# Softmax denominators transposed before the reciprocal, and one rounding of V moved to GpSimd

## The chip, the cores and the metric

The kernel runs on one core of a Trainium2 chip. The metric is the device time of one execution in microseconds (us); the number compared is the median of several executions. TensorE is called PE here, VectorE DVE, ScalarE ACT, GpSimd POOL, and SyncE, whose queue issues most DMAs, SP.

## What is computed

Rotary attention, then a gated feed-forward, then a second feed-forward with SoLU and layer norm. Only the attention is touched by the change:

```python
q_rot, k_rot = rotate(q), rotate(k)                      # batch 2, 8 heads, 576 rows, 64 columns
scores = q_rot @ k_rot.T / sqrt(64)
attn = exp(scores - max(scores))
attn = attn / (sum(attn) + 1e-09)
x = attn @ v                                             # then 1152 tokens x 512
x = (x @ w_a) * (x @ w_b) @ w_out
h = x @ moe2_w_in                                        # SoLU, layer norm, @ moe2_w_out
```

All of it is float32. Products run as float32r passes over a high part (the value rounded) and a low part (the rest) of each operand, so every operand is split by a copy ("high") and a subtraction ("low").

## The kernel before

**Tiling.** Two heads make a head pair; there are eight pairs, `u` = 0 to 7. A pair has nine blocks of 128 query rows: four of the first head, four of the second, and one (number 4) with the last 64 rows of both. For each block PE makes the scores `s` against all 576 keys (`qk`, L327), DVE takes the negated row maximum `nm` (L336), ACT takes the exponential `e` and adds up each row into one column of `sums[u]`, a tile of 128 partitions by 9 (L344), PE transposes `e` into `t` (L354), ACT copies it rounded into `pT` (L368) and DVE writes the low part (L372). The last 64 key rows are transposed apart (`t4A`, `t4R`, `t4B`, L378, evacuated at L386 and L390). Four products of `pT` with `V` (`pv`, L403), each evacuated by ACT (L410) and DVE (L417), give the pair's output `x0`, not yet divided.

**Division.** `rs_dve` (L422, L423) adds 1e-9 to the sums and takes their reciprocals on the 128 x 9 tile, in place. `rs_pe` (L427) transposes the result into PSUM, so that it has 9 partitions by 128. `rs_copy` (L430 to L446) copies it to SBUF on ACT as `rr`, and, for pairs 0 to 6, writes it to DRAM and reads it back three times, spread over the partitions, as `rb`; POOL then multiplies `x0` by `rb` (L468, L469) and takes the low part (L477). For the last pair `rb_pe` (L449) spreads `rr` with small products instead, and DVE multiplies (L483).

**V.** `v_hi` (L244) rounds the 128 x 640 tile `vraw` into the high half of `V` on DVE (L233); `v_lo` (L249) writes the low half on POOL (L251). POOL also does the rotation of keys and queries (L219 to L224), the low part of the keys (`k_lo`, L242), and the multiplications by `rb`.

**Order.** Nothing is scheduled by a tool: each part of a pair has a position in slots, nine slots a pair, in the tables `PLAN`, `FIRST`, `SECOND` and `THIRD`, where the last three override the first for pairs 0, 1 and 2. The parts are issued in the order of `9 * u + position`, and every engine works through its own instructions in that order. `rs` has three positions, for the sums' reciprocals, the transposition and the copy; `v_hi` and `v_lo` have one each. The last pair also has the first products of the feed-forward between its parts (`ab`, L579, at the positions in `AB`).

**Buffers.** The tiles with tag `o` in the pool `ps_o` share two PSUM buffers in rotation: the transpositions of queries and keys (`qtkA`, `qtqA`, `qtR`, `qtkB`, `qtqB`), `t4A`, `t4R`, `t4B`, `rs` and the four `pv`. Each of them waits until the one before the last has been evacuated. The scores `s` have two buffers, the transposed `t` two, and for the last pair the two tiles of `rb_pe` are taken from the buffers of `t`.

Of the kernel before, what the change touches and what calls it, by code (L numbers as in the profile page):

```python
# [15 lines left out]
ALU = mybir.AluOpType  # L16
# [4 lines left out]
B, H, S, D = 2, 8, 576, 64  # L21
NT, DM, DF1, DF2 = B * S, 512, 1536, 1024
P = 128
NP = H // 2
NU = B * NP
NB = 9
# [5 lines left out]
# When the parts of a head pair's work are issued, in slots from the pair's first one: each slot has  # L32
# the products of one block of queries, and the other parts are spread between them.
# [26 lines left out]
HI = {"k": "act", "v": "dve", "x": "pool", "l0": "pool", "l5": "dve", "q0": "dve", "q5": "dve", "r": "act"}  # L60
# [3 lines left out]
# A float64's high word is sign, 11 bits of exponent and 20 of mantissa. Read as a float32, the high  # L64
# words of the float32 range's ends are these two.
# [8 lines left out]
class Weights:  # L74
    """Float64 weights, as raw words in `raw` [P, n, 2], turned into float32 in `t` [P, n] and its
    float32r high and low parts in `w` [P, 2, n]; `scale` is a factor for each partition."""
# [4 lines left out]
    def pack(self, steps=range(5)):  # L81
        """The float32 value, cut to 24 bits; 0 below float32's range."""
        eng, t = self.nc.vector, self.t
        lo, hi = self.raw[:, :, 0], self.raw[:, :, 1]
        for step in steps:
            if step == 0:
                self.nc.scalar.activation(_raw(t), _raw(hi), AF.Abs)  # L87
            elif step == 1:
                eng.tensor_scalar(_raw(t), _raw(t), LOW_END, HIGH_END, op0=ALU.max, op1=ALU.min)  # L89
            elif step == 2:  # L90
                eng.tensor_scalar(t, t, 3, 0x3FFFFFFF, op0=ALU.logical_shift_left, op1=ALU.bitwise_and)  # L91
            elif step == 3:
                eng.scalar_tensor_tensor(t, hi, -(1 << 30), t, op0=ALU.bitwise_and, op1=ALU.bitwise_or)  # L93
            else:
                eng.scalar_tensor_tensor(t, lo, 29, t, op0=ALU.logical_shift_right, op1=ALU.bitwise_or)  # L95
# [12 lines left out]
def attention_gated_ffn_solu_ffn(ctx: ExitStack, tc, q, k, v, wa, wb, wo1, wi2, wo2, gln, rope_cs, out):  # L108
    """Products run as float32r passes over exact high and low halves of every float32 operand."""
    nc = tc.nc  # L110
# [12 lines left out]
    # ---- weights, in the order of their use: wa|wb by 128 columns, wo1 by 128 columns and half its  # L123
    # rows, wi2 by 128 rows and half its columns, wo2 (times the layer norm's factors) by 128 rows
# [39 lines left out]
    # ================= attention =================  # L164
# [14 lines left out]
    def load(u, nm_, parts="ABR", eng=nc.sync):  # L179
        """Queries or keys [P, 9, D]: 4 blocks of the first head's first 512 rows (row 4p + c is in  # L180
        block c), both heads' last 64 rows, 4 blocks of the second head's. Queries go into the second
        half of a tile [P, 9, 2, D], which will have them twice."""
        b, h0 = u // NP, 2 * (u % NP)
        if nm_ == "k":
# [3 lines left out]
            t = kraw[u]  # L188
# [55 lines left out]
    def v_hi(u):  # L244
        t = at.tile([P, 2, 5, 2, D], F32R, tag="V", name=f"V{u}")
        copy(HI["v"], t[:, :, :, 0, :].rearrange("p h c d -> p (h c) d"), vraw[u].rearrange("p h c d -> p (h c) d"))
        V[u] = t
# [173 lines left out]
    def rs_dve(u, key):  # L421
        nc.vector.tensor_scalar(sums[u], sums[u], 1e-9, None, op0=ALU.add)  # L422
        nc.vector.reciprocal(sums[u], sums[u])  # L423

# [5 lines left out]
    def rs_copy(u, key):  # L430
        rr = st.tile([NB, P], F32, tag="rr", name=f"rr{u}", bufs=2)
        copy(HI["r"], rr, po[u, key][0:NB, 0:P])
# [16 lines left out]
    def rb_pe(u):  # L449
        """1 / sum at every row of x0, by products with copies of the identity's columns."""  # L450
# [38 lines left out]
    # ---- what the start needs beside the plan  # L489
# [5 lines left out]
    def start():  # L495
# [19 lines left out]
        # the tensor engine's clock rises while it is busy: products of no use until the data is there  # L515
# [18 lines left out]
    for u in range(NU):  # L534
        plan = {key: tuple(9 * u + x for x in np.atleast_1d(pos)) for key, pos in PLAN.items()}
        for first, early in enumerate((FIRST, SECOND, THIRD)):
            if u == first:
                plan |= {key: tuple(9 * u + x for x in np.atleast_1d(pos)) for key, pos in early.items()}
# [22 lines left out]
        for keys, fns in (  # L561
            (("kA", "kB"), (qt_pe, qt_act)), (("qA", "R", "qB"), (qt_pe, qt_act, qt_dve)),
            (("t4A", "t4R", "t4B"), (t4_pe, t4_act, t4_dve)), (("rs",), (rs_dve, rs_pe, rs_copy)),
# [6 lines left out]
    # ================= first feed-forward: g = (x wa) * (x wb), transposed =================  # L570
# [27 lines left out]
    # the first two blocks of weights and their first products run beside the last head pair  # L598
# [36 lines left out]
    def load_after(n):  # L635
        """The loads that the raw words of block n have kept waiting."""
# [28 lines left out]
    # blocks 2 to 14 are prepared beside these products, in four steps each  # L665
# [4 lines left out]
    for i, (f, t) in enumerate(groups):  # L670
        # the last head pair's part comes last
# [7 lines left out]
    # ================= x2 = g wo1, transposed =================  # L679
# [42 lines left out]
    # ================= h = x2 wi2, solu, layer norm, out = ln wo2 =================  # L722
# [58 lines left out]
    def rows(i):  # L781
        """(partition range, rows of out) that the columns of token tile i stand for."""
# [90 lines left out]
```

## Time and profile before

| | us |
|---|---|
| median of three timed executions | 529.15 |
| lowest, highest | 528.02, 531.27 |
| span of the profiled execution, first to last instruction | 527.8 |

The profile comes from one execution of its own. A line such as "PE 492.1 (93%) x2992" is the busy time of an engine, its share of the span and its instructions. The attention takes the first 180 us; from there PE runs feed-forward products to the end. Line numbers (L422) are those of the kernel before. "DVE pT L372" is an instruction by engine, by the tile it writes and by its line; an "idle ... <-" part tells what ended the wait before it. Instructions on one engine can overlap by a tenth of a microsecond, since each is shown with its whole latency.

### The profile page before, as it was taken

How to read it: one execution, taken by the hardware profiler on the slowest of the kernel's cores; microseconds unless marked ns; L12 is line 12 of the kernel's file. 1: busy time of each engine (PE TensorE's matmuls, PEld its weight loads, DVE VectorE, ACT ScalarE, POOL GpSimd, SP SyncE). 2: the span in 40 equal slices, each digit the busy share in tenths (PEclk: the TensorE clock that was granted, in tenths of full speed). 3: DMA queues.
4: the chain of work that ended last, by engine and by line, in shares of the span. 5: the costliest groups of instructions: out<-in, count | busy, mean ns of one | idle time of the engine just before them, and what ended most of it. 6: DMA issues, size and time to landing. Idle time of an engine off the chain costs nothing.

```text
span 527.8 us, 7980 instructions
## 1 busy us (share of the span) xinstructions
PE 492.1 (93%) x2992; PEld 463.5 (88%) x2992; DVE 391.3 (74%) x603; ACT 271.0 (51%) x554; POOL 179.7 (34%) x128
## 2 busy tenths in 40 slices
PE   4889989989989999999999999999999489999997
PEld 4778888989878999999999999999999368888886
DVE  5899999999999766666656755746899986645440
ACT  2698988989898444343443333323445532222221
POOL 5598987787145003111222211220144330000000
PEclk9699999999999999999999999999999979999999
DMA  6344224225003044222332111334535100000011
GB/s 144 77 96 103 66 63 105 71 68 151 23 2 104 21 155 145 80 81 81 108 117 74 61 61 60 120 119 161 161 120 159 41 0 21 20 21 20 21 39 40
DMA packets 50914, 41.97 MB, mean 80 GB/s; under 512 B 23765, under 2 KB 46868, under 8 KB 50876
## 3 DMA queue, kind: packets, MB, share of 16 engines
q1 hardware_dynamic: 50124, 40.48, 25.6%
q10 hardware_dynamic: 624, 0.82, 0.5%
q8 instruction: 23, 0.38, 0.3%
q0 software_dynamic: 128, 0.17, 0.2%
q14 instruction: 15, 0.12, 0.1%
HBM read 37.00 MB, written 2.39 MB: 75 GB/s over the span
## 4 chain that ended last, share of the span: by engine, by line
PE 73%; DVE 18%; ACT 5%; issue 2%; DMA 1%; POOL 0%; DVEq 0%; ACTq 0%; POOLq 0%
PE ab L579 29%; PE x L710 10%; PE out L804 9%; PE h L735 8%; PE pv L403 6%; PE s L327 5%; PE t L354 3%; DVE f L95 3%; DVE nm L336 2%; ACT e L344 2%; DVE f L93 2%; DVE f L91 2%; DVE pT L372 2%; PE lt L775 1%; DVE f L89 1%
## 5 line engine op out<-in xcount | busy, mean ns | idle before, releaser
L579 PE MATMUL ab<-xT,wab 128*128 128x384 f32 x864 | 151.9, 336 | 0.0
L579 PEld LDWEIGHTS ab<-xT,wab 128*128 128x128 f32 x864 | 150.7, 188 | 0.1
L710 PE MATMUL x<-gT,wx 128*128 128x384 f32 x432 | 75.7, 336 | 0.0
L710 PEld LDWEIGHTS x<-gT,wx 128*128 128x128 f32 x432 | 75.6, 188 | 0.0
L104 POOL TENSOR_TENSOR wab<-f,wab 128x1024 fp32r<-128x1024 f32 x11 | 26.4, 2400 | 118.9 <-ACT wab L101 75.6
L735 PE MATMUL h<-wh,xT 128*128 128x512 f32 x216 | 54.4, 410 | 9.3 <-DVE et L753 9.3
L327 PE MATMUL s<-kS,qS 128*128 128x288 f32 x320 | 60.0, 315 | 1.2 <-ACT e L344 1.2
L735 PEld LDWEIGHTS h<-wh,xT 128*128 128x128 f32 x216 | 42.5, 198 | 19.7 <-issue 9.7
L344 ACT ACTIVATE e<-s,nm 128x576 f32<-128x576 f32 x72 | 53.6, 745 | 7.2 <-DVE nm L336 6.5
L336 DVE TENSOR_REDUCE nm<-s 128x1 f32<-128x576 f32 x72 | 53.7, 746 | 2.1 <-PE s L327 1.2
L804 PE MATMUL out<-wout,lnT 128*128 128x512 f32 (+1 forms) x240 | 52.9, 373 | 0.0
L372 DVE TENSOR_TENSOR pT<-t,pT 128x512 fp32r<-128x512 f32 x72 | 49.4, 686 | 2.5 <-ACT pT L368 1.4
L327 PEld LDWEIGHTS s<-kS,qS 128*128 128x128 f32 x320 | 47.3, 195 | 3.7 <-ACT e L344 3.0
L804 PEld LDWEIGHTS out<-wout,lnT 128*128 128x128 f32 x240 | 41.4, 188 | 7.4
L403 PE MATMUL pv<-pT,V 128*128 128x288 f32 x288 | 46.0, 304 | 0.9 <-DVE pT L390 0.9
L354 PE MATMUL t<-ident,e 128*128 128x128 f32 x288 | 44.3, 277 | 0.0
L368 ACT CAST pT<-t 128x512 fp32r<-128x512 f32 x72 | 42.2, 586 | 2.5 <-PE t L354 2.3
L403 PEld LDWEIGHTS pv<-pT,V 128*128 128x128 f32 x288 | 39.4, 188 | 2.0 <-POOL V L251 0.8
L587 ACT COPY a<-ab 128x384 f32<-128x384 f32 x36 | 17.3, 480 | 45.2 <-PE ab L579 44.6
L596 DVE TENSOR_TENSOR gT<-a,gT 128x384 fp32r<-128x384 f32 x36 | 23.1, 642 | 21.8 <-ACT gT L595 21.8
L95 DVE SCALAR_TENSOR_TENSOR f<-raw,f 128x512 int32<-128x512 int32 (+2 forms) x36 | 38.4, 1068 | 0.8
L89 DVE TENSOR_SCALAR f<-f 128x512 f32<-128x512 f32 (+2 forms) x36 | 29.4, 817 | 12.3 <-ACT f L87 12.2
(132 smaller groups left out, 689.2 us busy)
## 6 DMA issues: line engine op xcount, KB each, us to landing
raw<-in_moe_w_a_dram SPq DMA_DIRECT2D x12, 512.0 KB
raw<-in_moe_w_b_dram SPq DMA_DIRECT2D x12, 512.0 KB
raw<-in_moe_w_out_dram SPq DMA_DIRECT2D x8, 768.0 KB
raw<-in_moe_w_in_dram SPq DMA_DIRECT2D x8, 512.0 KB
raw<-in_moe_w_out_dram SPq DMA_DIRECT2D x8, 512.0 KB
kraw<-in_k_dram SPq DMA_DIRECT2D x16, 128.0 KB
vraw<-in_v_dram SPq DMA_DIRECT2D x8, 256.0 KB
qd<-qd SPq DMA_DIRECT2D x7, 288.0 KB
```

The lines of the kernel that those rows point to most:

```text
L95: eng.scalar_tensor_tensor(t, lo, 29, t, op0=ALU.logical_shift_right, op1=ALU.bitwise_or)
L327: nc.tensor.matmul(s[:, c, :KC], qS[u % 2][:, a, off:off + P], kS[u % 2][:, h, c * KC:(c + 1) * KC], start=(m == 0), stop=(m == last),)
L336: nc.vector.tensor_reduce(t, ps[n][:, :, :KC], axis=AX.XY, op=ALU.max, negate=True)
L344: nc.scalar.activation(t.rearrange("p (c n) -> p c n", c=2), ps.pop(n)[:, :, :KC], AF.Exp, bias=nm.pop(n), accum_out=sums[u][:, i:i + 1],)
L354: nc.tensor.transpose(t[:, j, :], e[n][:, j * P:(j + 1) * P], ident)
L368: nc.scalar.copy(hi, src)
L372: nc.vector.tensor_tensor(lo, src, _raw(hi), op=ALU.subtract)
L403: nc.tensor.matmul(o[:, :KC], w[:, h, 4 if m == 8 else m % 4].rearrange("p a d -> p (a d)"), t[:, m, c * KC:(c + 1) * KC], start=(m == 0), ...
L579: nc.tensor.matmul(pab[f, t][:, m, :CW], wf[:, a, m, kk, :], xT[:, kk, xa, t * CW:(t + 1) * CW], start=(kk == a == xa == 0), stop=(kk == 3 ...
L710: nc.tensor.matmul(o[:, :CW], wx[:, a], gT[f // 3, t][:, f % 3, ga], start=(f == 0 and a == ga), stop=(f == NF - 1 and a == 1),)
L735: nc.tensor.matmul(s[:, c], x2T[:, kk, xa, c0:c0 + P], wt["h", kk][:, a, c * 512:(c + 1) * 512], start=(idx == 0), stop=(idx == 11),)
L804: nc.tensor.matmul(o[:, cols], t[:, la, kk, :], w[:, a, cols], start=(kk == la == a == 0), stop=(kk == NK2 - 1 and la == 1),)
```

## The change

The sums are transposed as they are, and DVE then adds 1e-9 and takes the reciprocal on the 9 x 128 tile, reading the first from PSUM; ACT's copy is gone. So `rs` has two positions instead of three. From pair 2 on, `v_hi` is done by POOL, right ahead of `v_lo`; pairs 0 and 1 keep DVE. Comments are also gone, which shifts some line numbers by two to four.

```diff
-    "rs": (9.2, 10.3, 10.45), "pv00": ...
+    "rs": (9.9, 10.15), "pv00": ...
...
FIRST:
-    "v_lo": 5.0, ... "rs": (9.5, 10.3, 10.45),
+    "v_lo": 5.0, ... "rs": (9.9, 10.15),
...
-HI = {"k": "act", "v": "dve", "x": "pool", "l0": "pool", "l5": "dve", "q0": "dve", "q5": "dve", "r": "act"}
+HI = {"k": "act", "v": "pool", "x": "pool", "l0": "pool", "l5": "dve", "q0": "dve", "q5": "dve"}
...
     def v_hi(u):
-        copy(HI["v"], t[:, :, :, 0, :]..., vraw[u]...)
+        copy("dve" if u < 2 else HI["v"], t[:, :, :, 0, :]..., vraw[u]...)
...
-    def rs_dve(u, key):
-        nc.vector.tensor_scalar(sums[u], sums[u], 1e-9, None, op0=ALU.add)
-        nc.vector.reciprocal(sums[u], sums[u])
-
     def rs_pe(u, key):
         o = ps_o.tile([P, 512], F32, tag="o", name=f"rs{u}")
         nc.tensor.transpose(o[0:NB, 0:P], sums.pop(u), ident)
         po[u, key] = o
 
-    def rs_copy(u, key):
+    def rs_dve(u, key):
         rr = st.tile([NB, P], F32, tag="rr", name=f"rr{u}", bufs=2)
-        copy(HI["r"], rr, po[u, key][0:NB, 0:P])
+        nc.vector.tensor_scalar(rr, po[u, key][0:NB, 0:P], 1e-9, None, op0=ALU.add)
+        nc.vector.reciprocal(rr, rr)
...
         for first, early in enumerate((FIRST, SECOND, THIRD)):
+            if u > 1:
+                plan["v_hi"] = (plan["v_lo"][0] - 0.01,)
...
-            ... (("rs",), (rs_dve, rs_pe, rs_copy)),
+            ... (("rs",), (rs_pe, rs_dve)),
```

What the tables do to the order is seen in three places. On DVE, around the reciprocals of pair 4 (`sums` is the 128 x 9 tile, `rr` the 9 x 128 one, `x_4` the evacuation of a `pv`, `nm` a row maximum), the kernel before has:

```order
L372 TENSOR_TENSOR pT<-t_1614,pT 128x4x128
L422 TENSOR_SCALAR sums_1381<-sums_1381 128x9
L423 RECIPROCAL sums_1381<-sums_1381 128x9
L336 TENSOR_REDUCE nm_1659<-s_1637 128x1
L417 TENSOR_TENSOR x_4_1630<-pv_1622,tmp4pv_1649 64x288
L372 TENSOR_TENSOR pT<-t_1644,pT 128x4x128
L282 SCALAR_TENSOR_TENSOR qS_94<-qtqB_1651,qS_94 128x512
L336 TENSOR_REDUCE nm_1683<-s_1669 128x1
```

and the kernel after, at the same place:

```order
L372 TENSOR_TENSOR pT<-t_1608,pT 128x4x128
L336 TENSOR_REDUCE nm_1653<-s_1633 128x1
L417 TENSOR_TENSOR x_4_1626<-pv_1616,tmp4pv_1645 64x288
L372 TENSOR_TENSOR pT<-t_1640,pT 128x4x128
L282 SCALAR_TENSOR_TENSOR qS_94<-qtqB_1647,qS_94 128x512
L429 TENSOR_SCALAR rr_1679<-rs_1662 9x128
L430 RECIPROCAL rr_1679<-rr_1679 9x128
L336 TENSOR_REDUCE nm_1688<-s_1665 128x1
```

The two small instructions have moved four places back, behind the low part of `qtqB`, and work on 128 elements of a row instead of 9. On PE, for the same pair, the kernel before has the transposition `rs` behind `qtkA`, with `t4B` behind it:

```order
L265 MATMUL qtqB_1651<-ident,qd_1075 128x128 x4
L327 MATMUL s_1669<-kS_97,qS_94 128x288 x4
L354 MATMUL t_1678<-ident,e_1642 128x128 x4
L259 MATMUL qtkA_1685<-ident_r,kd_1493 128x128 x4
L427 MATMUL rs_1690<-ident,sums_1381 9x128
L378 MATMUL t4B_1693<-ident,e_1550 64x128
```

and the kernel after has it three groups earlier:

```order
L265 MATMUL qtqB_1647<-ident,qd_1071 128x128 x4
L423 MATMUL rs_1662<-ident,sums_1378 9x128
L327 MATMUL s_1665<-kS_97,qS_94 128x288 x4
L354 MATMUL t_1674<-ident,e_1638 128x128 x4
L259 MATMUL qtkA_1690<-ident_r,kd_1489 128x128 x4
L378 MATMUL t4B_1696<-ident,e_1544 64x128
```

With the two buffers of tag `o`, `rs` before waited for the evacuation of `qtqB`, and now waits for that of the `pv` ahead of `qtqB`; `qtkA` now waits for that of `qtqB`, and `t4B` for `rr`'s first instruction. On PE at the end of the last pair (`rb` are the products that spread `rr`, `ab` the first products of the feed-forward) the kernel before has:

```order
L579 MATMUL ab_0_2466<-xT,wab_1932 128x384 x6
L354 MATMUL t_2474<-ident,e_2453 128x128 x4
L579 MATMUL ab_0_2466<-xT,wab_1932 128x384 x3
L427 MATMUL rs_2482<-ident,sums_2236 9x128
L579 MATMUL ab_0_2466<-xT,wab_1932 128x384 x3
L378 MATMUL t4B_2487<-ident,e_2379 64x128
L378 MATMUL t4B_2487<-ident,e_2401 64x128
L378 MATMUL t4B_2487<-ident,e_2429 64x128
L378 MATMUL t4B_2487<-ident,e_2453 64x128
L456 MATMUL rb_0_2495<-rr_2493,ident 64x128 x8
L456 MATMUL rb_1_2496<-rr_2493,ident 64x64 x2
L403 MATMUL pv_2512<-pT,V_2102 128x288 x9
```

and the kernel after:

```order
L579 MATMUL ab_0_2457<-xT,wab_1927 128x384 x6
L423 MATMUL rs_2464<-ident,sums_2230 9x128
L354 MATMUL t_2467<-ident,e_2446 128x128 x4
L454 MATMUL rb_0_2475<-rr_2472,ident 64x128 x8
L454 MATMUL rb_1_2476<-rr_2472,ident 64x64 x2
L579 MATMUL ab_0_2457<-xT,wab_1927 128x384 x6
L378 MATMUL t4B_2493<-ident,e_2372 64x128
L378 MATMUL t4B_2493<-ident,e_2394 64x128
L378 MATMUL t4B_2493<-ident,e_2422 64x128
L378 MATMUL t4B_2493<-ident,e_2446 64x128
L403 MATMUL pv_2504<-pT,V_2184 128x288 x9
```

`rb` has moved ahead of six `ab` products and of `t4B`, so only the last transposition of `e` stands between `rs` and `rb`. POOL has six casts more, each directly ahead of the `V` subtraction of its pair; ACT has eight copies less; SP's order is the same.

## Rows read from the trace of the kernel before

**Rows 1.** The page, busy time by engine

```profile
PE 492.1 (93%) x2992; PEld 463.5 (88%) x2992; DVE 391.3 (74%) x603; ACT 271.0 (51%) x554; POOL 179.7 (34%) x128
```

**Rows 2.** Busy by stretch: PE, PEld, DVE, ACT, POOL, then clock, DMA share, GB/s

```profile
40.00:65.00 25.00, 23.38 (x186) 22.40 (x186) 24.03 (x41) 22.16 (x54) 22.13 (x17) 1.00 0.30 77
...
115.00:140.00 25.00, 22.56 (x180) 21.36 (x179) 24.05 (x42) 22.64 (x56) 15.56 (x11) 1.00 0.33 95
```

**Rows 3.** Chain that ended last, 113 to 118 us: start, length, work

```profile
113.84 1.06 DVE sums L422
...
116.70 0.61 DVE qS L282
...
117.35 0.28 PE rs L427
117.63 0.44 PE t4B L378 x4
```

**Rows 4.** Who waited for whom, 40 to 165 us: total, times, longest

```profile
PE rs L427 <- DVE qS L282: 3.0, 5, 0.6
PE t4B L378 <- ACT rr L231: 1.9, 1, 1.9
```

**Rows 5.** Groups by line and shape: busy us, mean ns

```profile
L233 DVE CAST V<-vraw 128x640 fp32r<-128x640 f32 x8 | 6.2, 778 | 0.0
L422 DVE TENSOR_SCALAR sums<-sums 128x9 f32<-128x9 f32 x8 | 6.2, 770 | 0.2
...
L282 DVE SCALAR_TENSOR_TENSOR qS<-qtR,qS 128x128 fp32r<-128x128 f32 x8 | 2.3, 282 | 0.0
...
L423 DVE RECIPROCAL sums<-sums 128x9 f32<-128x9 f32 x8 | 1.7, 216 | 0.3
...
L752 DVE RECIPROCAL sm<-sm 128x1 f32<-128x1 f32 x9 | 1.5, 164 | 0.3
```

**Rows 6.** Single lines: duration ns min/median/max, first and last start

```profile
L422 DVE TENSOR_SCALAR sums<-sums x8: 174/804/1544, 37.3 to 171.9; 128x9 f32<-128x9 f32 x8
L233 DVE CAST V<-vraw x8: 482/660/1159, 26.1 to 144.8; 128x640 fp32r<-128x640 f32 x8
```

**Rows 7.** Timeline of DVE, then of POOL, 86 to 96 us: start, length

```profile
87.50 1.15 DVE L233 CAST V<-vraw 128x640 fp32r<-128x640 f32 x1
...
95.17 0.56 DVE L422 TENSOR_SCALAR sums<-sums 128x9 f32<-128x9 f32 x1
...
86.88 1.43 POOL L468 TENSOR_TENSOR xT<-x,rb 128x576 fp32r<-128x576 f32 x1 [1.32 <-DVE x L417]
...
94.28 1.42 POOL L219 TENSOR_TENSOR t2k<-kraw,cs 128x576 f32<-128x576 f32 x1
```

**Rows 8.** Timeline around pair 4's sums and pair 5's keys, POOL, PE, DVE

```profile
113.44 1.41 POOL L242 TENSOR_TENSOR kd<-kraw,kd 128x576 fp32r<-128x576 f32 x1
...
114.23 0.60 PE L265 MATMUL qtqB<-ident,qd 128*128 128x128 f32 x4
...
116.25 0.51 PE L259 MATMUL qtkA<-ident_r,kd 128*128 128x128 f32 x4 [0.45 <-POOL t2k L219]
...
115.66 0.44 DVE L417 TENSOR_TENSOR x<-pv,tmp4pv 64x288 f32<-64x288 f32 x1
```

**Rows 9.** Group of POOL's subtraction on V: busy us, mean ns

```profile
L251 POOL TENSOR_TENSOR V<-vraw,V 128x640 fp32r<-128x640 f32 x8 | 12.6, 1569 | 0.0
```

**Rows 10.** Chain that ended last, end of the last pair, and one DVE instruction there

```profile
172.98 0.44 PE t L354 x4
173.42 0.53 PE ab L579 x3
173.95 0.11 PE rs L427
...
175.02 1.62 PE rb L456 x19
...
172.96 0.69 DVE L372 TENSOR_TENSOR pT<-t,pT 128x512 fp32r<-128x512 f32 x1 [0.16 <-ACT pT L368]
```

More of the change, by code (lines that the diff above doesn't have):

```diff
@@ L245, in v_hi @@
         t = at.tile([P, 2, 5, 2, D], F32R, tag="V", name=f"V{u}")
-        copy(HI["v"], t[:, :, :, 0, :].rearrange("p h c d -> p (h c) d"), vraw[u].rearrange("p h c d -> p (h c) d"))
+        copy("dve" if u < 2 else HI["v"], t[:, :, :, 0, :].rearrange("p h c d -> p (h c) d"), vraw[u].rearrange("p h c d -> p (h c) d"))
         V[u] = t
@@ L562, in attention_gated_ffn_solu_ffn @@
             (("kA", "kB"), (qt_pe, qt_act)), (("qA", "R", "qB"), (qt_pe, qt_act, qt_dve)),
-            (("t4A", "t4R", "t4B"), (t4_pe, t4_act, t4_dve)), (("rs",), (rs_dve, rs_pe, rs_copy)),
+            (("t4A", "t4R", "t4B"), (t4_pe, t4_act, t4_dve)), (("rs",), (rs_pe, rs_dve)),
             (("pv00", "pv01", "pv10", "pv11"), (pv_pe0, pv_pe1, pv_act, pv_dve)),
```

4 rows, old and new, of tables (FIRST, PLAN) are left out of this document.

## The prediction

> **What bounds the kernel now.** I read the page first, for which engine is full, then the busy time by stretch, then the chain that ended last, and only then single instructions. On the page PE is busy for 93% of the span [rows 1], which says nothing about the attention. The stretches do: between 40 and 140 us DVE is busy for 24.0 of 25 us, 96%, while PE has 22.6 to 23.4, ACT 22.2 to 22.6 and POOL 15.6 to 22.1, at a granted clock of 1.00 [rows 2]. So in the attention DVE is the fullest engine, and the others are close behind. A lighter DVE is worth something, but at most until PE or ACT is late in its place. The chain shows the place of the change on the path: at 113.84 us it goes through the two small instructions on the sums, on through a row maximum and the low part of `qtqB` on DVE, and from there to PE's `rs`, which could not start before that low part was written, because the buffer of `qtqB` was still full [rows 3]. PE waited for this 3.0 us in five pairs, and in one more 1.9 us at `t4B` for ACT's copy [rows 4].
>
> **What is removed on DVE.** The eight additions on 128 x 9 take 6.2 us and the eight reciprocals 1.7 us, 7.9 us together [rows 5]. The addition has nine elements a row and takes from 0.17 to 1.54 us [rows 6]. The timeline shows what it waits for: the one at 95.17 ended at 95.73, and POOL's instruction that began at 94.28 ended at 95.70; in the same way the cast of `V` at 87.50 ended 0.34 us after POOL's instruction (88.65 against 88.31) [rows 7]. These DVE instructions sit out a POOL instruction, and this goes with them. In the last pair POOL is idle and the two take only 0.17 + 0.22 = 0.39 us [rows 5, 6]. So pairs 0 to 6 lose 7.9 - 0.4 = 7.5 us. Of the casts of `V` those of pairs 2 to 7 go: four are at the row's minimum of 0.48 and two as long as the one at 87.50, 1.15 us, which makes 4.2 us [rows 6, 7]. Removed before the tail: 11.7 us of DVE's time.
>
> **What is added on DVE.** Per pair an addition that reads 128 elements from PSUM and a reciprocal of 128 elements; the trace shows neither.
>
> The addition: an instruction of DVE on 128 elements from PSUM takes 0.28 us [rows 5], and I take that. The bounds are 0.17 (the shortest of the old ones) and 1.54 us (if it should still wait for POOL) [rows 6]. If it waited as the old ones did on average (0.77), it would add 7 x 0.5 = 3.4 us. The Trainium skill ("VectorE: DVE Perf Modes", section "Why PSUM operands drop a tier") says that an operand in PSUM rules out the mode with two SBUF ports, and "GPSIMD Engine Reference", section 8, that this mode is one in which the two engines contend; by these the addition takes 0.28 whatever POOL does, which no row here shows.
>
> The reciprocal matters most. One element a row takes 164 ns and nine take 216 ns [rows 5]. The difference of 52 ns for eight elements is 6.5 ns an element, far more than the pass of 128 elements in 282 ns allows (under 2.2 ns). On the line through the two rows 128 elements cost 164 + 127 x 6.5 = 990 ns. The transposition spreads the same 1152 values over 9 rows instead of 128, and if each element costs 6.5 ns this is the dear layout. The lower bound is 0.3 us, if the reciprocal goes through its elements as fast as the other instructions do. The upper bound by plain proportion would be 216 x 128 / 9 = 3.07 us, but the row with one element shows that at least 164 ns of the 216 do not grow, so I exclude it and keep about 1.2. I take 0.99.
>
> Added to pairs 0 to 6: 7 x (0.28 + 0.99) = 8.9 us. DVE's balance there is 8.9 - 11.7 = -2.8 us. DVE is idle for 4% of these stretches, waiting for others, so a lighter DVE will wait a little more. I count three quarters, **-2.1 us** (half to all: -1.4 to -2.8).
>
> **What moves on PE in pairs 0 to 6.** `rs` now waits for the evacuation of the `pv` ahead of `qtqB` and stands in front of four products of scores and four transpositions. In pair 4 PE is through with `qtqB` at 114.23 + 0.60 = 114.83. That evacuation began at 115.66, behind the two instructions on the sums; without their 1.27 us it would begin at 114.4 and end at 114.8 [rows 3, 5, 8]. So I expect a wait of no more than 0.3 us, and none that counts, since DVE has the row maxima to catch up with. `qtkA` then waits for the low part of `qtqB` as `rs` did, and `t4B` for the new addition, which comes directly behind it. The old wait of 0.6 us is thus passed through about as before, only with more PE work done ahead of it. I book no gain of its own: it is the way in which DVE's gain reaches the chain.
>
> **ACT** loses eight small copies. It is not the engine that the chain waits for, save for the 1.9 us in one pair [rows 4]; there DVE's instructions run on, so I book nothing.
>
> **POOL** gets six casts of 128 x 640. A subtraction of this size takes 1.57 us [rows 9]; a copy reads one operand instead of two, so I bound it by half of that, 0.8 us, and the whole. They hide in the slack to the next user: `k_lo`, two places behind, ended at 113.44 + 1.41 = 114.85, and `qtkA`, which reads its result, began at 116.25 [rows 8], 1.4 us later. POOL's series also begins 0.5 us earlier, as it waits for an evacuation on DVE that stood behind the cast [rows 7]. If this cover were gone, each 0.1 us beyond 1.9 would cost 0.1 us in each of at most four pairs. I book nothing.
>
> **The tail of the last pair.** Here PE has no gap, and the change makes one. Before, three `ab` products, `rs`, three more and `t4B` stood between the last transposition and `rb`, and covered the reciprocals [rows 10]. Now PE goes from `rs` and the last transposition directly to `rb`, which needs `rr`. The low part at 172.96 ended at about 173.6; then 0.28 for the addition and 0.99 for the reciprocal, to 174.87. PE is free at 173.42 + 0.11 for `rs` = 173.53 [rows 10]. It waits 1.34 us. What follows (`rb`, six `ab`, `t4B`, `pv`) is the same work in another order, but `t4B` now stands directly in front of the `pv` whose last product needs its two evacuations, another 0.1. From there PE runs to the feed-forward without a gap, so all of it arrives at the end: **+1.4 us**, in general the reciprocal's time + 0.45.
>
> **The sum.** -2.1 + 1.4 = -0.7 us. Against the profiled execution this is 527.8 - 0.7 = 527.1 us of span; the median of the timed executions, 529.15, lies 1.35 above that span, and I carry this over: 528.45, rounded to **528.5 us**.
>
> **Rivals.**
>
> *The reciprocal is cheap.* It runs at the pace of other instructions, 0.3 us. For it speaks that an addition also grows between one element and nine, so the 52 ns may not be all per element. Against it, 52 ns is what the two rows show. DVE then has 7 x 0.58 = 4.1 us added and 7.6 removed net; three quarters are 5.7; the tail costs 0.75. Total -4.9: **524.2 us**.
>
> *The reciprocal is dearer than the line*, 1.2 us. For it speaks that the line rests on a difference of 52 ns between two very short instructions, where 10 ns more make 0.16 us at 128 elements; against it, only that the rows give 0.99. Added 7 x 1.5 = 10.5, net -1.2, of which 0.9 count; the tail 1.65. Total +0.8: **529.9 us**. The Trainium skill ("VectorE: DVE Perf Modes", section "Walkthrough: the 8-slice pipeline in each mode") says that the reciprocal is an iterative division with a repeat count of eight; at eight steps of its 0.96 GHz clock an element would cost 8.3 ns, and 128 of them 1.2 us, by my estimate. By that rule eight more elements should have cost 67 ns, and the trace shows 52.
>
> *PE stalls at the early transposition, and the kernel gets slower.* If DVE does not run ahead, the evacuation stays at 115.66 + 0.44 = 116.10, and PE waits 1.27 us in every pair, with the scores queued behind. Seven pairs make 8.9 us; the old waits of 4.9 go [rows 4]; DVE's gain doesn't reach the chain; the tail adds 1.4. Total +5.4: **534.5 us**. For it speaks that PE is the second fullest engine; against it, that all that stood between has left that place on DVE. It decides from 0.5 us a pair: 7 x 0.5 + 1.4 equals the 4.9 that go.
>
> **How the numbers follow.** A measurement of this kernel can tell about 1%, 5.3 us, from no change. I give the forecast 0.50 (its own range 527 to 529.5), the cheap reciprocal 0.20, the dear one 0.18, the stall on PE 0.07, and 0.05 to the rest, such as a late POOL. Faster by over 1% means under 523.9: half of the cheap case and a little of others, 0.12. Slower by over 1% means over 534.4: half of the stall and a little of the rest, 0.05. Within 1%: 0.83. The range of 8 in 10 goes from just below the cheap case, 523.5, to 532.0, between the dear case and the stall.
>
> **What would show it.** The reciprocal on 9 x 128 at 0.9 to 1.1 us, the addition ahead of it at 0.25 to 0.3 and nearly constant; `rs` waiting under 0.3 us in pairs 1 to 5; casts of `V` on POOL of 0.8 to 1.6 us without a wait of `qtkA` for POOL; a gap of PE of 1.2 to 1.5 us ahead of `rb`; and the products of the feed-forward starting about 0.7 us earlier than before. A reciprocal under 0.6 us, or waits of PE at `rs` over 0.5 us, would make the forecast wrong.

## The result and the profile after

| | before | changed |
|---|---|---|
| median of four timed executions, us | 528.81 | 532.17 |
| lowest, highest, us | 528.02, 531.27 | 531.52, 533.23 |
| ratio to before, 95% interval | | 1.0053 [1.0032, 1.0074] |
| span of the profiled execution, us | 527.8 | 531.5 |
| time of that execution, us | | 533.23 |

The changed kernel is 0.5% slower: less than the 1% that were called a difference, but surely on the slow side, and 0.17 us above the upper end of the forecast's range. Timed again beside another set of runs of before (the last experiment below) it gave 1.0067 [1.0041, 1.0092]. The ratio is an estimate over the executions of both kernels, not the quotient of the two medians, which is 1.0064.

The page of the changed kernel answers to [rows 1], and its first stretch to [rows 2] (columns as there):

```profile
PE 496.7 (93%) x2992; PEld 464.3 (87%) x2992; DVE 389.6 (73%) x597; ACT 269.2 (51%) x546; POOL 183.6 (35%) x134
```

```profile
40.00:65.00 25.00, 23.80 (x182) 21.89 (x181) 23.62 (x40) 22.73 (x55) 23.12 (x18) 1.00 0.32 82
```

DVE is lighter, as meant: 23.6 of 25 us where it had 24.0. But no other engine has become the full one in its place; all four have some air. That is the picture of a chain that goes round through several engines, not of one engine that is full. The lines of the new instructions (duration in ns, minimum/median/maximum, then first and last start) answer to [rows 6] and to the subtraction in [rows 9]:

```profile
L429 DVE TENSOR_SCALAR rr<-rs x8: 269/269/271, 39.0 to 174.2; 9x128 f32<-9x128 f32 x8
...
L430 DVE RECIPROCAL rr<-rr x8: 941/941/942, 39.3 to 174.5; 9x128 f32<-9x128 f32 x8
...
L233 POOL CAST V<-vraw x6: 711/714/723, 53.5 to 149.4; 128x640 fp32r<-128x640 f32 x6
```

The addition takes 0.27 us and is constant to 2 ns, the reciprocal 0.94 us, the cast on POOL 0.71 us. The waits between 40 and 165 us (waiting engine and line, what it waited for, total, times, longest) answer to [rows 4]; in the changed kernel:

```profile
ACT kS L302 <- PE qtkA L259: 4.7, 6, 0.8
...
PE rs L423 <- DVE x L417: 2.0, 6, 0.3
```

and, in the kernel before, the line that answers to the first of these:

```profile
ACT kS L302 <- PE qtkA L259: 0.5, 3, 0.2
```

PE's old wait at `rs` (3.0 us, five times) has become one of 0.33 us in each of six pairs. But it now stands ahead of the scores, which therefore begin 0.96 us behind the start of `qtqB` (114.71 - 113.75); before it was 0.36 us (114.59 - 114.23). New is a wait of ACT at its copy of `qtkA` (L302): 4.7 us where it had been 0.5. The timelines of PE and ACT at the place of [rows 8] (start, length, and in brackets the idle time before it and what ended it) show it for one pair:

```profile
113.75 0.60 PE L265 MATMUL qtqB<-ident,qd 128*128 128x128 f32 x4
...
114.68 0.28 PE L423 MATMUL rs<-ident,sums 128*9 128x128 f32 x1 [0.33 <-DVE x L417]
114.71 0.78 PE L327 MATMUL s<-kS,qS 128*128 128x288 f32 x4
...
116.00 0.51 PE L259 MATMUL qtkA<-ident_r,kd 128*128 128x128 f32 x4
...
116.55 0.59 ACT L302 CAST kS<-qtkA 128x512 fp32r<-128x512 f32 x1 [0.79 <-PE qtkA L259]
```

and the line of the scores in the kernel before:

```profile
114.59 0.78 PE L327 MATMUL s<-kS,qS 128*128 128x288 f32 x4
```

The chain of work that ended last, at the place of [rows 3] (start, length, work):

```profile
115.17 0.68 DVE qS L282
115.85 0.20 DVE rr L429
116.05 0.02 issue
116.08 0.04 DVE rr L430
116.11 0.83 issue
116.94 0.69 DVE nm L336
117.64 0.02 issue
117.66 0.84 ACT e L344 x2
118.50 0.04 issue
118.55 0.80 PE s L327 x4
```

Before, the chain left DVE at the low part of `qtqB` (`qS`, L282) for PE's `rs`. Now it stays on DVE: behind that low part come the addition and the reciprocal, then the row maximum, ACT's exponential and PE's scores. The 0.83 us of "issue" lie under the reciprocal, which began at 116.08 and takes 0.94.

Where the span grew, by PE's timeline in the two profiles:

| stretch on PE, us | before | changed | difference |
|---|---|---|---|
| to the first `qtqB` | 23.37 | 23.77 | +0.40 |
| first to third `qtqB` | 32.93 | 32.49 | -0.44 |
| third to eighth `qtqB` (five pairs) | 96.23 | 95.82 | -0.41 |
| eighth `qtqB` to the `pv` at 167.90 (168.52) | 15.37 | 16.44 | +1.07 |
| on to the end of the six `ab` at 172.98 (173.59) | 5.08 | 5.07 | -0.01 |
| from there to the end of the last `pv` | 6.77 | 10.10 | +3.33 |
| the rest, feed-forward | 348.05 | 347.81 | -0.24 |
| span | 527.8 | 531.5 | +3.7 |

The long steady part gains 0.85 us and pair 6 behind it gives back 1.07; the tail loses 3.33.

### The profile page after: what moved, and what is told of

Read it like the earlier page. It is cut to its first block, busy times and chain, and to the rows that moved or that the text cites. A ratio compares the mean times of both kernels' runs of the same rounds, so it can differ in the third digit from the quotient of the medians.

```text
span 531.5 us, 7960 instructions
## 1 busy us (share of the span) xinstructions
PE 496.7 (93%) x2992; PEld 464.3 (87%) x2992; DVE 389.6 (73%) x597; ACT 269.2 (51%) x546; POOL 183.6 (35%) x134
## 4 chain that ended last, share of the span: by engine, by line
PE 76%; DVE 16%; ACT 5%; issue 2%; DMA 1%; POOL 0%; DVEq 0%; POOLq 0%; ACTq 0%
PE ab L579 29%; PE x L710 9%; PE out L804 9%; PE h L735 8%; PE pv L403 7%; PE s L327 6%; PE t L354 3%; DVE nm L336 3%; DVE f L95 3%; ACT e L344 2%; DVE f L93 2%; DVE f L91 2%; PE lt L775 1%; DVE f L89 1%; DMA qd<-in_q_dram 1%
```

## The experiments

Two figures recur below. *Five pairs* is the time from the third to the eighth `qtqB` on PE, as in the table: 96.23 us before, 95.82 in the changed kernel. *Lag* is the time from the start of the sixth `qtqB` to the start of ACT's copy of the `qtkA` behind it: 116.80 - 114.23 = 2.57 us before, 116.55 - 113.75 = 2.80 in the changed kernel. Before, `qtkA` itself came late there, behind a wait of PE of 0.45 us that the profile puts down to POOL [rows 8]; from the third `qtqB` on the lag was 2.09 to 2.58 us there, and the last two of the five pairs already took 19.1 to 19.2 us each, as all five do in the changed kernel.

Each ratio below is to executions of the kernel before that were timed beside that run. Their medians are 529.00 us for e1 to e4, 529.85 for e5 to e8 and 529.61 for e9 to e12, so runs of different groups are compared by ratio and not by time.

### The tail, and each part by itself

**e1.** `rb` of the last pair goes back behind the six products of the feed-forward and `t4B`; all else is the changed kernel.

```diff
-            add(plan["rs"][-1] + 0.02, rb_pe, u)
+            add(plan["rs"][-1] + 0.32, rb_pe, u)
```

> The changed kernel with one position altered: in the last pair the products that spread the reciprocals stand behind the six ab products and t4B again, as in the kernel before. Theory A (the tail makes most of the loss: PE waits 1.44 us for the 9 x 128 reciprocal, and the granted clock then falls and makes the next products slow): the wait and the slow products go, the time is 3.0 to 3.5 us below the changed kernel, about 528.7, the same as before within 0.5 us. Theory B (the loss is in pairs 0 to 6, where the reciprocal stands in front of a row maximum): the tail gives back at most 1 us, about 531.

Measured: 529.22 us, 0.9998 [0.9983, 1.0013]. The wait at `rb` is gone. So the tail costs 1.0053 - 0.9998 = 0.55%, 2.9 us, not 1.4; and the pairs before it, which were to gain 2.1 us, gain nothing in sum, to within the interval of 0.8 us either way (five pairs 95.84, lag 2.80). Both terms of the sum are off.

**e2.** The wait for `rr` stays, but PE is kept busy in it with twelve products of no use.

```diff
+    def busy(u):
+        t = ps_o.tile([P, 512], F32, tag="o", name="busy")
+        for i in range(12):
+            nc.tensor.transpose(t[:, i % 4 * P:(i % 4 + 1) * P], ident, ident)
...
+            add(plan["rs"][-1] + 0.01, busy, u)
```

> The changed kernel with twelve transpositions of the identity, of no use, put into the gap of PE ahead of the spreading products, so that PE works through the 1.3 us while the reciprocal runs; nothing else is moved. If the granted clock answers to the gap: PE's wait stays as work, but the six ab products behind take about 1.1 us and not 2.1, t4B 0.44 and not 0.85; the time is 1.5 to 2.0 us below the changed kernel, about 530.3, and 1.2 to 1.6 above the one with the tail covered. If the slow products have another cause (the order of the work, the weights), they stay slow and the time is that of the changed kernel, 532.2, or a little more.

Measured: 531.61 us, 1.0040 [1.0025, 1.0055]. It lies below the changed kernel, but the intervals overlap; the profiles of the tails, under e4, say more.

**e3.** Only `V`'s rounding goes to POOL; the sums stay as they were before.

```diff
-        copy(HI["v"], t[:, :, :, 0, :]..., vraw[u]...)
+        copy("dve" if u < 2 else "pool", t[:, :, :, 0, :]..., vraw[u]...)
...
+            if u > 1:
+                plan["v_hi"] = (plan["v_lo"][0] - 0.01,)
```

> The kernel before with one part of the change: the cast of V on POOL from pair 2 on; sums, reciprocals and tail as before. DVE loses 4.2 us. By the prediction's term (three quarters of what DVE loses are gained): 3.1 us faster, 525.7. If PE and ACT are late in its place and the pairs keep their period of about 19.16 us: the two long casts at 68 and 87 us, which sat out a POOL instruction, still give 0.6 us each, about 527.3 in all. If POOL becomes late: slower than 528.8.

Measured: 525.41 us, 0.9923 [0.9901, 0.9945], faster than both kernels; five pairs 92.52, lag 1.90.

**e4.** Only the sums' part: `V` is rounded on DVE in all pairs.

```diff
-        copy("dve" if u < 2 else HI["v"], t[:, :, :, 0, :]..., vraw[u]...)
+        copy("dve", t[:, :, :, 0, :]..., vraw[u]...)
...
-            if u > 1:
-                plan["v_hi"] = (plan["v_lo"][0] - 0.01,)
```

> The changed kernel with V cast on DVE again at the old places: the other part alone. Theory A: the tail's 3.3 us stay, the reciprocal of 0.94 us with the addition of 0.27 replaces about as much on DVE, and the casts cost what they did: 532.5 to 533.5. Theory B': the two parts don't add, the cast on POOL gave nothing, and the time is that of the changed kernel, 532.2.

Measured: 533.74 us, 1.0081 [1.0065, 1.0098]; five pairs 97.68. One part gains 0.8%, the other loses as much; the two together would make 1.0004 if they added up, and the changed kernel has 1.0053. The parts do not add up. One reason is that they partly save the same thing. The additions on the 128 x 9 tile in e3 (duration ns, as in [rows 6]):

```profile
L422 DVE TENSOR_SCALAR sums<-sums x8: 173/174/1420, 37.6 to 168.3; 128x9 f32<-128x9 f32 x8
```

The median is 174 ns where it was 804, and the eight take 3.6 us instead of 6.2. The timeline of e3, DVE and then POOL, shows why at one of them:

```profile
111.78 0.17 DVE L422 TENSOR_SCALAR sums<-sums 128x9 f32<-128x9 f32 x1
...
110.31 1.57 POOL L251 TENSOR_TENSOR V<-vraw,V 128x640 fp32r<-128x640 f32 x1
111.84 1.42 POOL L242 TENSOR_TENSOR kd<-kraw,kd 128x576 fp32r<-128x576 f32 x1
```

With the cast on POOL its instructions are shifted against DVE's, and the addition at 111.78 falls into the seam between two of them (111.88 and 111.84). Five of eight wait for nothing, where two did before (those of the last two pairs). Of what the sums' part was to save on DVE, the waits on POOL, more than half is thus gone already, and 0.17 + 0.22 us are exchanged for 0.27 + 0.94.

The tail, PE's timeline from the last `rs` on. The changed kernel:

```profile
173.42 0.27 PE L423 MATMUL rs<-ident,sums 128*9 128x128 f32 x1
...
175.57 1.66 PE L454 MATMUL rb<-rr,ident 9*64 9x128 f32 x20 [1.44 <-DVE rr L430]
177.16 2.16 PE L579 MATMUL ab<-xT,wab 128*128 128x384 f32 x6
179.12 1.05 PE L378 MATMUL t4B<-ident,e 128*64 128x128 f32 x4
```

and e4, with the same wait:

```profile
177.29 1.66 PE L454 MATMUL rb<-rr,ident 9*64 9x128 f32 x20 [1.43 <-DVE rr L430]
178.88 1.34 PE L577 MATMUL ab<-xT,wab 128*128 128x384 f32 x6
180.06 0.60 PE L378 MATMUL t4B<-ident,e 128*64 128x128 f32 x4
...
182.05 0.40 PE L403 MATMUL pv<-pT,V 128*128 128x288 f32 x1 [0.33 <-DVE pT L390]
```

The stretch behind the wait, in the changed kernel and then in e4 (busy time of PE, PEld, DVE, ACT, POOL, then the granted clock):

```profile
178.00:180.00 2.00, 2.00 (x10) 1.75 (x9) 0.00 (x0) 0.00 (x0) 0.00 (x0) 0.50 0.00 0
```

```profile
178.00:180.00 2.00, 2.00 (x22) 1.93 (x18) 0.29 (x1) 0.00 (x0) 0.00 (x0) 1.00 0.00 0
```

In the changed kernel the granted clock has fallen to 0.50, which is 1.2 instead of 2.4 GHz, after PE stood for 1.44 us (the wait ended at 175.57, and the clock is at 0.50 from about 177.5 to 180.5); the same six `ab` products take 2.16 us instead of 1.34, and `t4B` 1.05 instead of 0.60. In e4 the clock stayed at 1.00 behind a wait of 1.43 us. From the end of the six `ab` products ahead of `rs` to the end of the last `pv` it is the same work but for e2's additional products, in another order:

| | before | e1 | e2 | e4 | changed |
|---|---|---|---|---|---|
| us | 6.77 | 6.76 | 8.87 | 8.88 | 10.10 |

So the wait costs 8.88 - 6.77 = 2.1 us (1.43 at `rb`, 0.33 more at the last `pv` product for the low part of `t4B`, the rest in the seams), and the lower clock another 1.2 us in this execution. With PE kept busy (e2) the clock did not fall; but it did not fall in e4 either, so one profile of e2 doesn't show that the additional work prevented it.

### Where the gain of the pairs went

After e1, e3 and e4 two causes were open for the pairs: the reciprocal of 0.94 us on DVE, or the place of `rs`, which makes ACT wait at its copy of `qtkA`.

**e5.** e1, and the reciprocal moved behind the next row maximum (the addition keeps its place, to free the buffer).

```diff
-        nc.vector.reciprocal(rr, rr)
         po[u, "rr"] = rr
+    def rs_rec(u, key):
+        rr = po[u, "rr"]
+        nc.vector.reciprocal(rr, rr)
...
+        plan["rs"] += (9*u + (10.95 if u < NU - 1 else 10.16),)
...
-            add(plan["rs"][-1] + 0.02, rb_pe, u)
+            add(plan["rs"][-1] + 0.31, rb_pe, u)
```

> The changed kernel with the tail covered, and in pairs 0 to 6 the reciprocal of 9 x 128 alone three places further back on DVE, behind the next row maximum and low part (position 10.95); the addition, which frees the PSUM buffer, stays. Theory A (place: the reciprocal is dear because a row maximum stands behind it, which ACT's exponential and PE's next scores wait for): 0.3 to 0.5 us a pair back, 526 to 527. Theory B (load: 0.87 us of DVE cost as much anywhere): no change from the kernel with the tail covered, 529.2.

Measured: 534.66 us, 1.0081 [1.0054, 1.0109]; five pairs 99.81, lag 2.80. Worse: the reciprocal now stands in front of the next row maximum and of `t4B`'s low part, for which PE's `pv` waits.

```profile
PE pv L403 <- DVE pT L390: 6.2, 6, 1.0
```

This was 0.3 us in two pairs in the kernel before. The reciprocal is no cheaper there.

**e6.** e3, with the addition as a sum of two tiles, the sums and a constant tile of 1e-9.

```diff
+    eps = const.tile([P, NB], F32, name="eps")
...
-        nc.vector.tensor_scalar(sums[u], sums[u], 1e-9, None, op0=ALU.add)
+        nc.vector.tensor_tensor(sums[u], sums[u], eps, op=ALU.add)
```

> The kernel before with the cast of V on POOL from pair 2 on, and the addition of 1e-9 on 128 x 9 written as a sum of two SBUF tiles, sums and a constant, in place of tensor_scalar; places and reciprocals as before. In the run with V alone seven of the eight additions took 0.17 us and one, of pair 0, 1.42. If a sum of two SBUF tiles doesn't sit out a POOL instruction: all eight at about 0.2 us, 0 to 1 us below the run with V alone, about 525. If it does sit them out: as the run with V alone or slower.

Measured: 525.00 us, 0.9917 [0.9886, 0.9949], not to be told from e3. The expectation misread e3, in which five additions took 0.17 us and not seven. In e6 it is five as well, two take 0.65 and 0.67 us, and the first takes 1.54.

**e7.** The same edit of the addition on the kernel before, and nothing else.

> The kernel before with that sum of two tiles in place of tensor_scalar alone; V stays on DVE. It takes away what the additions sat out, 6.2 - 8 x 0.2 = 4.6 us of DVE, and nothing else. If DVE's time at this place is worth about half to all of itself: 2.3 to 4.6 us faster, 524.5 to 526.7. If the addition's wait is covered (PE or ACT late anyway): 528.5 to 529. If the sum of two tiles waits for POOL too: 529 or more, with additions over 0.5 us.

Measured: 528.99 us, 0.9984 [0.9971, 0.9996]. The addition waits as before:

```profile
L423 DVE TENSOR_TENSOR sums<-sums,eps x8: 170/795/1423, 37.3 to 171.7; 128x9 f32<-128x9 f32 x8
```

So the form with two tiles sits out POOL's instructions too, and is no way round them.

**e8.** e1 without the reciprocals of pairs 0 to 6.

```diff
-        nc.vector.reciprocal(rr, rr)
+        if u == NU - 1:
+            nc.vector.reciprocal(rr, rr)
```

> The changed kernel with the tail covered, without the reciprocals of pairs 0 to 6 (their x is multiplied by the sums in place of divided by them); the last pair keeps its own. This takes 7 x 0.87 = 6.1 us from DVE between the low part of qtqB and a row maximum. If that place is on the path in every pair: 4.5 to 6 us below the kernel with the tail covered, 523 to 524.7. If PE or ACT is the limit of the pairs: 1 to 2 us, 527 to 528.

Measured: 528.15 us, 0.9957 [0.9941, 0.9972]; five pairs 95.88, lag 2.80. This run decides most. With 6.6 us of work taken off DVE (7 x 0.94, of which 4.7 in the five pairs) the five pairs take as long as with it, 95.88 against 95.84. Something else sets their pace. ACT's wait is still there, and DVE now stands for ACT's rounding of `t` instead, 6.3 us where it was 0.8 in the changed kernel:

```profile
ACT kS L302 <- PE qtkA L259: 4.0, 5, 0.8
...
DVE pT L372 <- ACT pT L368: 6.3, 10, 1.0
```

The chain of e8 goes through PE's wait at `rs` and then through that copy, where the changed kernel's goes through the reciprocal:

```profile
113.32 0.37 DVE x L417
...
113.73 0.28 PE rs L423
...
115.05 0.53 PE qtkA L259 x4
...
115.60 0.59 ACT kS L302
116.19 0.50 ACT pT L368
...
117.32 0.75 DVE nm L336
...
118.10 0.69 DVE pT L390
...
118.92 1.42 PE pv L403 x9
```

So both ways round the loop are about equally long, and taking one away leaves the other. What e8 gains over e1 is outside the five pairs: from the eighth `qtqB` to the `pv` behind pair 6 it takes 15.54 us, and e1 16.45. That is 0.9 of 2.2 us (0.41%); the profiles don't show where the rest of it is, and the two intervals are wide enough to hold it.

**e9.** e1, with the transposition of the sums of pairs 0 to 6 back at its old place, behind `qtkA`; the new reciprocal stays.

```diff
+        if u < NU - 1:
+            plan["rs"] = (9*u + 10.3, 9*u + 10.45)
```

> The changed kernel with the tail covered, and in pairs 0 to 6 the transposition of the sums on PE behind qtkA again (position 10.3; addition and reciprocal of 9 x 128 behind it, 10.45). With the early place qtkA takes the buffer that qtqB had, waits for DVE's low part, and ACT stands before its copy of qtkA for 0.8 us a pair. Theory A (the place on PE and so the rotation of the two buffers holds the pairs at 19.16 us): ACT's waits of 0.8 go, the period falls to 18.6 to 18.9, about 526.5. Theory B (the reciprocal of 0.94 us holds them, wherever the transposition stands): 528.5 to 530.

Measured: 528.74 us, 0.9984 [0.9967, 1.0000]; five pairs 95.19, lag 1.90. ACT's wait is gone, but now the reciprocal is on the path: PE's `pv` waits 2.7 us in six pairs for `t4B`'s low part, which stands behind it.

**e10.** e3 (old reciprocals on 128 x 9, old copy on ACT), with the transposition at the early place.

```diff
+        if u < NU - 1:
+            plan["rs"] = (plan["rs"][0], 9*u + 9.9, 9*u + 10.05)
```

> The run with V alone (525.4), with nothing but the place of the transposition altered in pairs 0 to 6: on PE directly behind qtqB as in the changed kernel (9.9), ACT's copy at 10.05; addition and reciprocal on 128 x 9 ahead of it as before. Theory A (rotation of the buffers): the period goes from 18.4 to about 19.1 and the time to 528.5 to 530, with ACT waiting 0.8 us a pair for qtkA, though no reciprocal of 9 x 128 is in it. Theory B (the reciprocal): 525 to 526, as with V alone.

Measured: 530.04 us, 1.0003 [0.9989, 1.0017]; five pairs 95.96, lag 2.64. With no reciprocal of 0.94 us anywhere, the early place alone takes the whole gain of e3 away (0.9923), and ACT waits at its copy again:

```profile
PE rs L427 <- DVE x L417: 3.7, 6, 0.9
...
ACT kS L302 <- PE qtkA L259: 2.4, 6, 1.0
```

But here the delay comes from `rs` alone. The evacuation of the `pv` that `rs` waits for stands behind the old addition and reciprocal on DVE, so PE stands at `rs` for 0.4 to 0.9 us a pair. `qtkA` then follows without a wait. It even begins (116.73) before DVE's low part of `qtqB` has ended (116.20 + 0.67 = 116.87), so in e10 it does not use that buffer; the two buffers are handed out in another order than in the changed kernel. PE, then DVE:

```profile
116.73 0.54 PE L259 MATMUL qtkA<-ident_r,kd 128*128 128x128 f32 x4
...
116.20 0.67 DVE L282 SCALAR_TENSOR_TENSOR qS<-qtqB,qS 128x512 fp32r<-128x512 f32 x1
```

**e11.** e8 and e9 together: the old place, and no reciprocals in pairs 0 to 6.

> The kernel with the transposition at the old place, without the reciprocals of pairs 0 to 6 (their x is multiplied by the sums in place of divided). Without them but with the early place the time was 0.4% under the kernel before, with a period of 19.17 us. Theory A: the period falls to 18.4 or under, 524 to 525; the difference to the run with the old place and the reciprocal is what 0.87 us on DVE cost there. Theory B: as with the early place, 527 to 528.

Measured: 523.59 us, 0.9888 [0.9864, 0.9912]; five pairs 91.97, lag 1.90. Against e8 nothing but the place of the transposition differs. PE's timeline in e11 and then in e8, whose `qtkA` begins at 115.05:

```profile
110.10 0.60 PE L265 MATMUL qtqB<-ident,qd 128*128 128x128 f32 x4
110.46 0.78 PE L327 MATMUL s<-kS,qS 128*128 128x288 f32 x4
...
111.42 0.54 PE L259 MATMUL qtkA<-ident_r,kd 128*128 128x128 f32 x4
```

```profile
112.80 0.60 PE L265 MATMUL qtqB<-ident,qd 128*128 128x128 f32 x4
...
113.77 0.78 PE L327 MATMUL s<-kS,qS 128*128 128x288 f32 x4
```

Counted from the start of `qtqB`, the scores begin 0.61 us later with the early place (0.97 against 0.36), because PE stands at `rs`, and `qtkA` 0.93 us later (2.25 against 1.32). The other 0.32 us are `qtkA`'s own wait for the low part of `qtqB`.

This completes a table of six, which all have `V` on POOL and a covered tail:

| reciprocals of pairs 0 to 6 | old place: ratio, five pairs | early place: ratio, five pairs |
|---|---|---|
| left out | 0.9888, 91.97 (e11) | 0.9957, 95.88 (e8) |
| on 128 x 9, as before | 0.9923, 92.52 (e3) | 1.0003, 95.96 (e10) |
| on 9 x 128, as changed | 0.9984, 95.19 (e9) | 0.9998, 95.84 (e1) |

The early place alone costs 0.7 to 0.8% (e8 - e11, e10 - e3; the intervals of each two lie apart). The reciprocal on 9 x 128 alone costs 0.96% against none (e9 - e11). Both together cost 1.1% (e1 - e11). They do not add up: each by itself makes five pairs last between 95.2 and 96 us, so undoing either one alone gains almost nothing in the steady part. The version to keep is e3: `V`'s move without the sums' part.

**e12.** The changed kernel again, without an edit.

> The changed kernel once more, as it is. In its first profile the granted clock was at 0.50 in 178 to 180 us, behind a wait of PE of 1.44 us; in the run with V on DVE the same wait left it at 1.00. If the fall comes in some executions only: a profile with clock 1.00 there, or a spread of the executions of more than 1 us; median 531.5 to 532.5. If it comes with the wait each time: 0.50 again.

Measured: 532.78 us, 1.0067 [1.0041, 1.0092]; five pairs 95.82, as in the first profile. The granted clock fell here too, behind a wait of 1.39 us at `rb`:

```profile
178.00:180.00 2.00, 2.00 (x10) 2.00 (x9) 1.38 (x2) 0.42 (x2) 0.00 (x0) 0.50 0.00 0
```

Its span is 528.6 us, 2.9 below that of the first profile, of which 1.6 are there at the third `qtqB` already (54.63 against 56.26); the tail from the six `ab` on takes 9.80 us. The start differs so much between executions of one kernel that two spans alone would have told nothing here.

## Why the prediction was wrong

**The durations were right.** Addition 0.28 forecast, 0.27 measured, and constant; reciprocal 0.99 and 0.94; PE's early wait "no more than 0.3 us", 0.33 measured (that it would not count was wrong, as below); POOL's cast, put between 0.8 and 1.57 us, takes 0.71, under the lower end, and no wait of `qtkA` for POOL came from it. The wait at `rb`, 1.34 forecast, was 1.44. The rivals of a cheap and of a dear reciprocal are out by the 941 ns alone. The line through two short rows held: (941 - 216)/119 = 6.1 ns an element, where it had 6.5. The Trainium skill ("VectorE: DVE Perf Modes", section "Walkthrough: the 8-slice pipeline in each mode") gives a repeat count of eight for the division; at eight steps of 1/0.96 ns each, by my estimate, an element would take 8.3 ns, and the trace shows 6.1. For the addition from PSUM the rule weighed in the prediction held: it does not wait for POOL, while a sum of two tiles in SBUF does (e7). The Trainium skill ("GPSIMD Engine Reference", section "8. Key points") names both cases, two-port modes and two SBUF inputs, and the trace agrees (the longest of these sums took 1.42 us).

**The failed step: the pairs, -2.1 us forecast, nothing measured (e1).** It failed in the paragraph on what moves on PE. There the wait at the early transposition is put at "no more than 0.3 us, and none that counts", the old wait of 0.6 us "is thus passed through about as before", and "I book no gain of its own: it is the way in which DVE's gain reaches the chain". The size of the wait was right, and so was the rotation in the changed kernel: `rs` takes one of the two buffers ahead of `qtkA`, so that `qtkA` waits for DVE's low part of `qtqB`, as `rs` did before. What was not asked is who stands behind. Behind `rs` at its old place it was ACT's small copy and `t4B`. At its early place the scores, a transposition and `qtkA` stand behind it, and behind `qtkA` ACT's copy `kS`. Since ACT works in order, its next rounding of `t`, its exponential and its rounding of `t4B` come after that copy, and with these DVE's low parts and PE's `pv`.

The lag shows the shift. At the sixth `qtqB` it is 1.90 us with the old place (e3, e9, e11; e3 has 2.17 and 2.18 in two other pairs) and 2.80 with the new one (changed, e1, e5, e8), whatever DVE has to do in between. Of these 0.90 us about two thirds come from PE's stand at `rs` and one third from `qtkA`'s wait for the low part (e8 against e11). In e10, with 2.64, all of it comes from the stand at `rs`. That the place costs the 0.7 to 0.8% is shown by e10 and e8; that it does so by this chain is read from the waits and from e8's chain. Pair 6, which has no `qtkA` behind it, fits this: PE waits at the early `rs` there too, 0.33 us in e8 and 0.46 in e10, but the stretch behind the eighth `qtqB` is as long with the early place as with the old one (15.54 us in e8 and in e11, 15.33 in e10 and 15.34 in e3). There PE stands at `t4B` a little later in any case (0.86 us in e8, 1.37 in e11), which takes the stand at `rs` up. Whether a third buffer would free it was not tried.

**Pair 6** shows the sums' part without its savings. There the old addition had waited for nothing (0.17 us at 152.16), so the change only adds: 0.27 + 0.94 for 0.17 + 0.22, 0.82 us, and they lie on the path: the stretch is 1.07 us longer, and without the reciprocal (e8) it is 15.54 us, 0.17 over the kernel before. The prediction's average over pairs 0 to 6 hid this.

**The three quarters.** The balance of DVE, -2.8 us, was right in kind: DVE did become lighter (391.3 us busy on the page before, 389.6 in the changed kernel, with the tail's addition and reciprocal in it). But the prediction took the fullest engine for the one that nearly sets the pace. With the early place the loop through `rs` and ACT's copy holds the pace at about 19.2 us a pair, and a lighter DVE is worth nothing: e8 takes 4.7 us off it in the five pairs, and they do not move.

**One quantity was counted in the wrong part.** The additions' waits for POOL (most of the 7.5 us that the prediction takes off DVE for additions and reciprocals) were booked as a gain of the transposed sums. The move of `V` alone shortens them (6.2 to 3.6 us in e3), so the sums' part had less left to save than it cost. Read separately, the change is one good edit (e3, 0.9923) and one bad one (e4, 1.0081).

**The tail, +1.4 forecast, 2.9 measured.** The mechanism was right, the term too small. The wait was 1.44 us as worked out; 0.33 us at the last `pv` product and some seams make it 2.1; and the clock, which the prediction did not ask about, adds 1.2 us in one profile of the changed kernel and 0.9 in the other (10.10 and 9.80 us against 8.88). Both profiles of the changed kernel show the fall, e4's not, with the same wait; what decides it is open. The two misses, 2.1 us in the pairs and 1.5 in the tail, put 528.5 up to 532.1, which is the measured time but for 0.1 us. That the change stayed within 1%, to which the prediction gave 0.83, therefore speaks for neither of its two terms.

**The rival of a stall on PE** (534.5 us) named the right edit, the early transposition, and the right sign, and with 0.07 got too little weight. Its mechanism was right in kind and too large. PE did not wait 1.27 us at `rs`, but 0.33, which put the scores back by 0.61 us a pair, over the 0.5 us from which, by the prediction, this rival decides. It lacked the second part, the wait of `qtkA`, and ACT's copy behind it.

## What to carry to other kernels

When a tile is put into a rotation of shared buffers at another place, list for each tile behind it whose evacuation it now waits for, and who stands in order behind its own evacuation: here a wait of a third of a microsecond cost nothing in pair 6, where PE had to wait a little later anyway, and held the loop back in the pairs where ACT waited for the next tile. Where a change has two parts, ask of every saving whether one part alone already brings it; and before an engine's balance is counted as time, look whether a second way round the loop is as long. The reciprocal here cost by its elements in a row, so take it in the layout with many partitions and few elements.

## What was not expected of the hardware

- DVE's reciprocal: 164 ns for one element a row, 216 for nine, 941 for 128; the same 1152 values cost 4.4 times as much on 9 rows as on 128.
- DVE's addition on an SBUF tile of 128 x 9 sits out what is left of a POOL instruction or nothing, so its length is set by phase: 0.17 us in a seam of POOL's work, up to 1.54 us outside it. With a cast of 0.71 us put into POOL's series (e3) five of eight fell free, where it had been two. The reciprocal on the same tile, right behind it, takes 0.22 us every time (215 to 217 ns in the kernel before).
- The granted clock went to 0.50 behind a gap of PE of 1.4 us in two executions of the changed kernel, and stayed at 1.00 behind the same gap in e4.
- Executions of one kernel differed by 1.6 us by the third head pair (changed kernel, 54.63 against 56.26).
